# A short convolution and an ELU layer: softmax on eight partitions, one load of w_in, the band in contiguous rows

## The chip, the cores and the metric

The kernel runs on one core of one Trainium2 chip. Its metric is the time of one execution on the device in microseconds; lower is better.

## The reference

`x` is (8, 4096, 192), `weight` is (8, 7): eight heads of 24 channels, seven taps each. A softmax over each head's taps gives the weights of a causal convolution along the sequence. Its output, seen as 32768 tokens of 192 channels, goes through two matrix products with an ELU between them.

```python
w = softmax(weight, axis=-1)                      # (8, 7)
x_pad = concat([zeros(B, 6, D), x], axis=1)
a[b, s, h, :] = sum_k w[h, k] * x_pad[b, s + k, h, :]
h = a.reshape(32768, 192) @ w_in                  # w_in (192, 2048)
g = where(h > 0, h, exp(min(h, 0)) - 1)
out = g @ w_out                                   # w_out (2048, 192)
```

## The kernel before

Tokens are worked through in 32 stages of 1024 (`SUP`), each as two groups of 512. The hidden dimension is cut into 16 blocks of 128 (`NQ`). The counter `n` runs over stage and block, 512 values in all. For each `n` and each group `r` TensorE makes one hidden tile of 128 x 512 in a PSUM bank, out of three accumulating matmuls of 64 rows ("h", L798). Group 0 uses partitions 0 to 63 of `w_in` and `att`, group 1 partitions 64 to 127, so that two matmuls run side by side in the two halves of the array. This is why `w_in` stands twice in SBUF, in the lower and in the upper half of the partitions.

A hidden tile then goes through three engines. ScalarE takes the exponential from PSUM to `E` (L606), GpSimd clamps it (L557), and VectorE makes the ELU from `E` and the PSUM bank and writes `gT` (L679), which frees the bank. TensorE multiplies `gT` by `w_out` ("o", L821).

The convolution of stages 1 to 31 is done on TensorE as a product of windows of `x` (`xg`) with a banded matrix `Tm` ("c", L773), four units of two heads per stage. ScalarE evacuates each unit (L602), and a transposing DMA on SP's queue puts a stage into `att`. Stage 0 has its own way, so that it can start early: ScalarE casts `xs` (L585), TensorE transposes it ("t", L723), VectorE and ScalarE copy the transposed tiles into `xT`, and TensorE multiplies them by `taps`, one diagonal matrix for each tap ("d", L751).

`Tm` is made from the softmax. VectorE writes the weights into `wband`, SP's queue writes `wband` to the DRAM tensor `conv_band` with one element more per row than the row is long, and reads it back shifted (L844, L853). SP waits for the first transfer before it issues the second. The first convolution unit stands in TensorE's order at n = 6 (`EARLY_CONV`), and waits for both transfers.

The order of TensorE's items is written out when the program is built, from a plan with a cost for each kind of item; engines run their lists in order and wait on semaphores. At the start stand `WARM[0]` matmuls on zeros ("w", L714), then `start_up`: transposes with one more matmul on zeros after each of three, and the "d" matmuls. Before each of n = 1 to 3 stands one more.

GpSimd makes the masks (`ident`, `band16`) and then issues the loads, which all go through one queue in this order: `w_in` columns 0 to 1023 into both halves (six DMAs), half of `w_out`, two of `xg`, `w_in` columns 1024 to 2047 into both halves (six DMAs), the rest of `w_out`, two of `xg`. Each of these DMAs also changes float32 to a 16-bit type. The load of `weight` and that of eight rows of `x` (`xh`) are SP's first two; that of `xs` is on ScalarE's queue.

Of the kernel before, what the change touches and what calls it, by code (L numbers as in the profile page):

```python
# [5 lines left out]
ALU = mybir.AluOpType  # L6
# [6 lines left out]
P = 128  # L13
HP = 64
# [22 lines left out]
QB = 2  # L37
WARM = (15, 1)
FILL = 1
WCOLS = ((0, 8 * FC), (8 * FC, 16 * FC))  # L40
HALO = 8
# [15 lines left out]
def bass_lightweight_conv__then__act_elu_kernel(  # L57
# [178 lines left out]
    emit(tail)  # L236
    pe_order.append(("w", 0, WARM[0]))
    for what in start_up:
# [44 lines left out]
    with ExitStack() as stack:  # L283
        def sbuf(name, shape, dt):
            return stack.enter_context(nc.sbuf_tensor(name, shape, dt))
# [4 lines left out]
        def sema(name):  # L290
            return stack.enter_context(nc.semaphore(name))

        xg = sbuf("xg", [P, NXB, 2 * NWIN, D], BF16)
        Tm = sbuf("Tm", [P, HEADS, CW], BF16)
        ident = sbuf("ident", [P, P], BF16)
# [6 lines left out]
        xb = sbuf("xb", [P, 3, XI, HP], BF16)  # L302
        own = sbuf("own", [P, HEADS], FP32)
        band16 = sbuf("band16", [P, 2 * HEADS], FP32)
        wown = sbuf("wown", [P, HEADS], FP32)
        wsel = sbuf("wsel", [P, KSIZE, HEADS], FP32)

# [6 lines left out]
        osb = sbuf("osb", [P, 2, 2, 2, D], FP32)  # L314
        wq = sbuf("wq", [P, HEADS, KSIZE], FP32)
        wmx = sbuf("wmx", [P, HEADS], FP32)
        wq2 = sbuf("wq2", [P, HEADS, KSIZE], FP32)
        wex = sbuf("wex", [P, HEADS, KSIZE], FP32)
        wsum = sbuf("wsum", [P, HEADS], FP32)
        wrs = sbuf("wrs", [P, HEADS], FP32)  # L320
        wband = sbuf("wband", [P, HEADS, BW], BF16)
        wch = sbuf("wch", [P, KSIZE], FP32)
        zw = sbuf("zw", [P, TW * HEADS], BF16)
        scr = sbuf("scr", [P, 2], FP32)
        H = psum("H", [P, NBANK, GS])

        s_wq = sema("s_wq")
        s_w = [sema(f"s_w{i}") for i in range(4)]
        s_set = sema("s_set")
# [5 lines left out]
        s_xh = sema("s_xh")  # L335
        s_own = sema("s_own")
        s_wb = sema("s_wb")
# [132 lines left out]
        def _gpsimd(g: bass.BassGpSimd):  # L470
# [28 lines left out]

            def load_w_in(k, half):  # L500
                c0, c1 = WCOLS[k]
                for j in range(3):
                    g.dma_start(  # L503
                        w_in[HP * half : HP * (half + 1), j, c0:c1],
                        bass.AP(
                            tensor=moe_w_in.tensor,
                            offset=8 * j * FF + c0,
                            ap=[[CPH * FF, HEADS], [FF, 8], [1, c1 - c0]],
                        ),
                    ).then_inc(s_w[k], 16)  # L510

            def load_w_out(k):
                q = slice(NQ // 2 * k, NQ // 2 * (k + 1))
                g.dma_start(
                    w_out[:, q, :], moe_w_out.rearrange("(q p) d -> p q d", p=FC)[:, q, :]
                ).then_inc(s_w[2 + k], 16)

# [11 lines left out]
            for step in range(2):  # L529
                W(s_id, 2 + step)  # L530
                g.affine_select(
                    out=band16[:],
                    in_=band16[:] if step else ones[:, 0 : 2 * HEADS],
                    pattern=[[8 * (2 * step - 1), 2 * HEADS]],
                    compare_op=ALU.is_ge,
                    fill=0.0,
                    base=7 * step,
                    channel_multiplier=1 - 2 * step,
                ).then_inc(s_id)
            load_w_in(0, 0)  # L540
            load_w_in(0, 1)
            load_w_out(0)
            for gr in range(2):
                load_x(1, gr)
            load_w_in(1, 0)
            load_w_in(1, 1)
            load_w_out(1)
# [67 lines left out]
        def _vector(v):  # L615
            W = Waits(v)
            v.memset(zw[:], 0.0).then_inc(s_zw)  # L617
            v.memset(wband[:], 0.0).then_inc(s_wb)
            v.memset(xbh[:, :, 0, :], 0.0).then_inc(s_xz)
            W(s_wb, 1)  # L620
            W(s_id, 4)
            v.tensor_tensor(own[:], band16[:, 0:HEADS], band16[:, HEADS : 2 * HEADS], ALU.add).then_inc(s_own)
            W(s_wq, 16)
            v.tensor_reduce(wmx[:], wq[:], AXIS.X, ALU.max).then_inc(s_set)  # L624
            W(s_set, 1)
            v.tensor_tensor(  # L626
                wq2[:],
                wq[:],
                wmx[:, :].unsqueeze(2).to_broadcast([P, HEADS, KSIZE]),
                ALU.subtract,  # L630
            ).then_inc(s_set)
# [4 lines left out]
            W(s_set, 4)  # L636
            W(s_own, 1)
            v.tensor_tensor(wown[:], wrs[:], own[:], ALU.mult).then_inc(s_set)
            W(s_set, 5)
            v.tensor_tensor(  # L640
                wsel[:],
                wex[:, :, :].rearrange("p h k -> p k h"),
                wown[:, :].unsqueeze(1).to_broadcast([P, KSIZE, HEADS]),
                ALU.mult,
            ).then_inc(s_set)
            W(s_set, 6)
            v.tensor_reduce(wch[:], wsel[:], AXIS.X, ALU.add).then_inc(s_set)
            W(s_set, 7)
            v.tensor_tensor(  # L649
                taps[:],  # L650
                ident[:, :].unsqueeze(1).to_broadcast([P, KSIZE, P]),
                wch[:, :].unsqueeze(2).to_broadcast([P, KSIZE, P]),
                ALU.mult,
            ).then_inc(s_tap)
            for at, j in enumerate((3, 0)):
                W(s_xt, at + 1)
                v.tensor_copy(*transposed(j)).then_inc(s_fd)  # L657
            v.tensor_tensor(
                wband[:, :, P - KSIZE : P][:, :, ::-1],
                wex[:, :, :],  # L660
                wrs[:, :].unsqueeze(2).to_broadcast([P, HEADS, KSIZE]),
                ALU.mult,
            ).then_inc(s_set)
            W(s_first, 2)
            v.tensor_copy(*first_att(1, 0, GS)).then_inc(s_fd)  # L665
            W(s_first, 3)
            v.tensor_copy(*first_att(2, GS // 2, GS)).then_inc(s_fd)
            for item in dve_order:
                if item[0] == "e":
                    v.tensor_copy(*out_evac(W, *item[1:])).then_inc(s_od)  # L670
                    continue
                _, n, u = item
                i = unit_at[n, u]
                s, q = divmod(n, NQ)
                if s >= NG3:
                    for g in range(2):
                        W(s_fin[g], 2 * (s - NG3 + 1))
                W(s_clp, i + 1)
                v.scalar_tensor_tensor(  # L679
                    out=gT[:, s % NG3, q, u, :],  # L680
                    in0=E[:, i % NE, :],
                    scalar=1.0,
                    in1=H[:, bank_of[item], :],
                    op0=ALU.subtract,
                    op1=ALU.max,
                ).then_inc(s_tt)

        @block.tensor
        def _tensor(pe):
# [16 lines left out]
            for item in pe_order:  # L706
                if item[0] == "w":
# [5 lines left out]
                    for _ in range(item[2]):  # L713
                        pe.matmul(H[:, bank, :], zw[:, 0:P], zw[:, 0:GS], start=True, stop=True)  # L714
                elif item[0] == "t":
                    j = item[1]
# [26 lines left out]
                elif item[0] == "d":  # L743
                    j = item[1]
                    W(s_tap, 1)
                    first_evacuated(W, ("t", j))
# [12 lines left out]
                elif item[0] == "c":  # L759
# [9 lines left out]
                    else:  # L769
# [4 lines left out]
                        H[0:CW, bank_of["c", m], 256 * q : 256 * q + UC],  # L774
                        Tm[rows, h, :],
                        xg[rows, s % NXB, :, CPH * h : CPH * (h + 1)].rearrange(
# [8 lines left out]
                elif item[0] == "h":  # L785
                    _, n, r, j = item
                    s, q = divmod(n, NQ)
                    if j == 0:
                        if q < WCOLS[0][1] // FC:
                            W(s_w[0], 96)  # L790
                        else:
                            W(s_w[1], 96)
                        if s:
                            W(s_att[s % 2], att_need(s))
                        wait_bank(item[:3])
# [12 lines left out]
                else:  # L808
# [7 lines left out]
                    if visit is not None and not opens:  # L816
                        W(s_turn[g], turns[k, g])
                    W(s_w[2 + q // (NQ // 2)], 16)
                    W(s_tt, tt_count(NQ * t + q, g))
# [16 lines left out]
        def _sync(sy):  # L836
            W = Waits(sy)
            sy.dma_start(
                wq[:, :, :].rearrange("p h k -> p (h k)"),
                bass.AP(tensor=weight.tensor, offset=0, ap=[[0, P], [1, HEADS * KSIZE]]),  # L840
            ).then_inc(s_wq, 16)
            sy.dma_start(xh[:, :], x_flat[GS - HALO : GS, :]).then_inc(s_xh, 16)
            W(s_set, 8)
            sy.dma_start(  # L844
# [8 lines left out]
            sy.dma_start(  # L853
                Tm[:, :, :],
                band[:, P - 1 : P - 1 + HEADS * BW].rearrange("p (h i) -> p h i", h=HEADS)[
                    :, :, 0:CW
                ],
            ).then_inc(s_band, 16)

            sync_work = []  # L860
# [39 lines left out]
```

## Time and profile before

| | |
|---|---|
| median of 9 runs | 734.33 us (733.53 to 734.9) |
| the profiled execution's own time | 734.4 us |
| its span, first to last instruction | 732.5 us |
| busy: PE, DVE, ACT, POOL | 721.6, 639.9, 677.5, 671.2 us |
| mean granted TensorE clock | 0.995 |
| HBM read, written | 36.20 MB, 25.66 MB |

PE is TensorE's matmuls, PEld its weight loads, DVE VectorE, ACT ScalarE, POOL GpSimd, SP SyncE; a name with q is an engine's sequencer, which issues DMAs. An arrow `a <- b` in a row of the waits means that a waited for b; then come the total in us, the number of times and the longest. In a row of the chain or of the timeline stand start, length in us, engine, tile and line. A row of the windows gives the stretch, its length, the busy time and the count of each engine, the granted clock as a share of full speed, the time of the DMA packets as a share of 16 engines (over 1 where packets overlap), and GB/s. Matmuls are pipelined, so a busy TensorE may still work below its peak.

### The profile page before, as it was taken

The numbers are of one execution on the slowest core, as the hardware profiler recorded it, in microseconds if no ns is written. First come the engines' busy times: TensorE is split into PE (matmuls) and PEld (weight loads), VectorE is DVE, ScalarE is ACT, GpSimd is POOL, SyncE is SP. The second block draws the span as 40 slices with busy tenths as digits, with TensorE's granted clock in tenths as the row PEclk, the third lists the DMA queues.
The fourth block names the chain that finished last, engine by engine and source line by source line (L and its number), as shares of the span: only waits on it lengthen the run. The fifth ranks groups of instructions, "written<-read, shape, count | busy, mean of one in ns | idle before, by whom it ended". The sixth has DMA issues, their size and how long they took to land.

```text
span 732.5 us, 27618 instructions
## 1 busy us (share of the span) xinstructions
PE 721.6 (99%) x11858; PEld 683.0 (93%) x11860; DVE 639.9 (87%) x1042; ACT 677.5 (92%) x1287; POOL 671.2 (92%) x1116
## 2 busy tenths in 40 slices
PE   8799999999999999999999999999999999999998
PEld 4479999999999999999999999999999999999997
DVE  3699899889899889899889898889898889898993
ACT  4699999999999999999999999999999999999993
POOL 7699999999999999999999999999999999999892
PEclk9899999999999999999999999999999999999999
DMA  9635455434445534545534455534445533545212
GB/s 188 81 51 94 72 95 85 85 52 92 76 92 85 79 66 84 75 92 85 95 51 83 80 88 86 95 59 75 83 84 85 95 63 70 93 75 84 69 34 67
DMA packets 133947, 59.40 MB, mean 81 GB/s; under 512 B 100024, under 2 KB 132800, under 8 KB 133824
## 3 DMA queue, kind: packets, MB, share of 16 engines
q1 hardware_dynamic: 88960, 39.07, 23.6%
q0 software_dynamic: 44448, 17.58, 22.7%
q8 instruction: 93, 1.52, 0.9%
q10 hardware_dynamic: 416, 0.98, 0.4%
q14 instruction: 30, 0.25, 0.1%
HBM read 36.20 MB, written 25.66 MB: 84 GB/s over the span
## 4 chain that ended last, share of the span: by engine, by line
PE 93%; DMA 3%; POOL 2%; ACT 1%; DVE 1%; issue 0%; DVEq 0%
PE H L821 53%; PE H L798 37%; PE H L773 3%; POOL E L557 1%; DMA Tm<-conv_band 1%; DMA conv_band<-wband 1%; DMA wq<-in_weight_dram 1%; ACT E L606 1%; POOL xg L485 0%; ACT csb L602 0%; DVE taps L649 0%; ACT osb L610 0%; DVE gT L679 0%; DVE xT L657 0%; DVE osb L670 0%
## 5 line engine op out<-in xcount | busy, mean ns | idle before, releaser
L679 DVE SCALAR_TENSOR_TENSOR gT<-E,H 128x512 f16<-128x512 f32 x1024 | 633.3, 683 | 71.7 <-POOL E L557 70.3
L821 PE MATMUL H<-w_out,gT 64*128 64x192 f16 x8192 | 685.3, 243 | 0.2
L798 PE MATMUL H<-att,w_in 64*128 64x512 bf16 x3072 | 683.4, 377 | 0.6 <-issue 0.3
L557 POOL TENSOR_SCALAR E<-E 128x512 f32<-128x512 f32 x1024 | 607.7, 614 | 48.0 <-ACT E L606 37.0
L821 PEld LDWEIGHTS H<-w_out,gT 64*128 64x128 f16 x8192 | 628.3, 94 | 21.0 <-PE H L821 2.6
L606 ACT ACTIVATE E<-H 128x512 f32<-128x512 f32 x1024 | 593.7, 601 | 34.0 <-PE H L798 8.2
L798 PEld LDWEIGHTS H<-att,w_in 64*128 64x128 bf16 x3072 | 275.2, 93 | 6.7 <-ACT csb L602 1.0
L773 PE MATMUL H<-xg,Tm 64*112 64x240 bf16 x496 | 93.4, 268 | 4.7 <-DMA Tm<-conv_band 4.2
L602 ACT ACTIVATE csb<-H 112x480 bf16<-112x480 f32 x124 | 70.0, 564 | 0.0
L610 ACT ACTIVATE osb<-H 128x384 f32<-128x384 f32 x127 | 61.7, 486 | 7.5 <-PE H L821 7.4
L773 PEld LDWEIGHTS H<-xg,Tm 64*112 64x112 bf16 x496 | 58.0, 127 | 8.7 <-DMA Tm<-conv_band 4.5
L485 POOL DMA_DIRECT2D xg<-in_x_dram x63 | 56.1, 896 | 0.2 <-issue 0.2
L714 PE MATMUL H<-zw 128*128 128x512 bf16 x19 | 7.6, 549 | 1.5 <-DVE zw L617 1.5
L714 PEld LDWEIGHTS H<-zw 128*128 128x128 bf16 x21 | 2.6, 130 | 6.4 <-issue 4.6
L670 DVE COPY osb<-H 128x384 f32<-128x384 f32 x1 | 0.6, 558 | 8.4 <-PE H L821 8.4
L503 POOL DMA_DIRECT2D w_in<-in_moe_w_in_dram x12 | 7.1, 669 | 0.0
L751 PE MATMUL H<-xT,taps 128*128 128x512 bf16 (+1 forms) x28 | 4.7, 325 | 0.0
L751 PEld LDWEIGHTS H<-xT,taps 128*128 128x128 bf16 x28 | 2.7, 97 | 2.0
L597 ACT ACTIVATE att<-H 128x512 bf16<-128x512 f32 (+1 forms) x2 | 1.0, 490 | 3.7 <-PE H L751 3.7
L576 ACT ACTIVATE wex<-wq 128x56 f32<-128x56 f32 x1 | 0.2, 249 | 4.0 <-DVE wq L626 4.0
L665 DVE CAST att<-H 128x512 bf16<-128x512 f32 x1 | 0.7, 692 | 3.6 <-PE H L751 3.6
L624 DVE TENSOR_REDUCE wmx<-wq 128x8 f32<-128x56 f32 x1 | 0.2, 211 | 3.7 <-DMA wq<-in_weight_dram 3.7
(34 smaller groups left out, 19.2 us busy)
## 6 DMA issues: line engine op xcount, KB each, us to landing
out_dram<-osb SPq DMA_DIRECT2D x127, 192.0 KB, 3.6
xg<-in_x_dram POOLq DMA_DIRECT2D x61, 240.0 KB, 5.0
w_in<-in_moe_w_in_dram POOLq DMA_DIRECT2D x12, 128.0 KB, 8.1
xs<-in_x_dram ACTq DMA_DIRECT2D x1, 768.0 KB, 6.6
w_out<-in_moe_w_out_dram POOLq DMA_DIRECT2D x2, 384.0 KB, 11.3
att<-csb SPq DMA_TRANSPOSE x31, 4.3
conv_band<-wband SPq DMA_DIRECT2D x1, 480.0 KB, 6.8
Tm<-conv_band SPq DMA_DIRECT2D x1, 224.0 KB, 8.9
```

Source lines behind the costliest of these rows:

```text
L485: g.dma_start(xg[0:rows, b, 2 * w0 + gr : 2 * w1 : 2, :], src).then_inc(s_x[b][gr], 16)
L503: g.dma_start(w_in[HP * half : HP * (half + 1), j, c0:c1], bass.AP(tensor=moe_w_in.tensor, offset=8 * j * FF + c0, ap=[[CPH * FF, HEADS], ...
L557: g.tensor_scalar(out=E[:, i % NE, :], in0=E[:, i % NE, :], scalar1=1.0, scalar2=0.0, op0=ALU.min, op1=ALU.max,).then_inc(s_clp)
L602: a.activation(*conv_evac(W, m), ACT.Copy).then_inc(s_ce)
L606: a.activation(E[:, i % NE, :], H[:, bank_of[item], :], ACT.Exp).then_inc(s_exp)
L610: a.activation(*out_evac(W, *item[1:]), ACT.Copy).then_inc(s_oev[item[2]])
L679: v.scalar_tensor_tensor(out=gT[:, s % NG3, q, u, :], in0=E[:, i % NE, :], scalar=1.0, in1=H[:, bank_of[item], :], op0=ALU.subtract, op1=A ...
L714: pe.matmul(H[:, bank, :], zw[:, 0:P], zw[:, 0:GS], start=True, stop=True)
L751: ins = pe.matmul(H[:, bank_of[item] + part, c0:c1], taps[:, tap, :], xT[:, j, HALO - PAD + tap + c0 : HALO - PAD + tap + c1], start=(tap ...
L773: ins = pe.matmul(H[0:CW, bank_of["c", m], 256 * q : 256 * q + UC], Tm[rows, h, :], xg[rows, s % NXB, :, CPH * h : CPH * (h + 1)].rearrang ...
L798: ins = pe.matmul(H[:, bank_of[item[:3]], :], w_in[HP * r : HP * (r + 1), j, FC * q : FC * (q + 1)], att[HP * r : HP * (r + 1), s % 2, j, ...
L821: ins = pe.matmul(acc_of(k, g)[:, D * kb : D * (kb + 1)], gT[HP * rt : HP * (rt + 1), t % NG3, q, g, t0 : t0 + P], w_out[HP * rt : HP * (r ...
```

## The change

The softmax is computed once, on eight partitions, one for each head, instead of on all 128. Two small matmuls spread it: one with the mask `owner` gives every partition the seven weights of its head (for `taps`), one with ones and a block-diagonal copy `wnb` gives every partition all 56 weights (for `wband`). VectorE reads both from PSUM. `wband` is written right after `taps`, ahead of the copies into `xT`. The matmuls on zeros at the start are 6, then the two small ones, then 4.

`w_in` is loaded into the lower half only, in three parts (columns 0 to 511, 512 to 1023, 1024 to 2047). VectorE copies the first two parts to the upper half, the third goes by a DMA from SBUF to SBUF on SP's queue. The hidden matmuls of group 1 wait for these copies.

`Tm` has rows of 240 columns per head instead of 112, so that the read of the band moves one contiguous row of 1792 elements to each partition; the matmuls use the first 112 columns.

```diff
-WARM = (15, 1)
+WARM = (6, 1, 4)
-WCOLS = ((0, 8 * FC), (8 * FC, 16 * FC))
+WCOLS = ((0, 4 * FC), (4 * FC, 8 * FC), (8 * FC, 16 * FC))
...
-    pe_order.append(("w", 0, WARM[0]))
+    pe_order += [("w", 0, WARM[0]), ("s",), ("w", 0, WARM[2])]
...
-        Tm = sbuf("Tm", [P, HEADS, CW], BF16)
+        Tm = sbuf("Tm", [P, HEADS, BW], BF16)
-        wq = sbuf("wq", [P, HEADS, KSIZE], FP32)
+        wq = sbuf("wq", [HEADS, KSIZE], FP32)
-        zw = sbuf("zw", [P, TW * HEADS], BF16)
+        zw = sbuf("zw", [P, GS], BF16)
...
 # GpSimd: two masks for owner (as before for band16), one more for block8, then
-            load_w_in(0, 0)
-            load_w_in(0, 1)
+            load_w_in(0)
+            load_w_in(1)
             load_w_out(0)
             for gr in range(2):
                 load_x(1, gr)
-            load_w_in(1, 0)
-            load_w_in(1, 1)
+            load_w_in(2)
             load_w_out(1)
...
 # VectorE
+            def upper_half(v, k):
+                c0, c1 = WCOLS[k]
+                W(s_w[k], 48)
+                v.tensor_copy(w_in[HP:P, :, c0:c1], w_in[0:HP, :, c0:c1]).then_inc(s_wc)
 # wmx, wq2, wex (ScalarE), wsum, wrs as before but on 8 partitions; then
-            v.tensor_tensor(wown[:], wrs[:], own[:], ALU.mult).then_inc(s_set)
-            v.tensor_tensor(wsel[:], wex..., wown..., ALU.mult).then_inc(s_set)
-            v.tensor_reduce(wch[:], wsel[:], AXIS.X, ALU.add).then_inc(s_set)
+            v.tensor_scalar(out=wn[:], in0=wex[:], scalar1=wrs[:, 0:1], ...)
+            v.tensor_tensor(wnb[:], block8[:], wn..., ALU.mult).then_inc(s_set)
+            W(s_sel, 1)
             v.tensor_tensor(
                 taps[:],
                 ident[:, :].unsqueeze(1).to_broadcast([P, KSIZE, P]),
-                wch[:, :].unsqueeze(2).to_broadcast([P, KSIZE, P]),
+                H[:, bank_of["d", 2], 0:KSIZE].unsqueeze(2).to_broadcast([P, KSIZE, P]),
                 ALU.mult,
+            ).then_inc(s_tap)
+            v.tensor_copy(
+                wband[:, :, P - KSIZE : P][:, :, ::-1],
+                H[:, bank_of["d", 2], HP : HP + HEADS * KSIZE]...,
             ).then_inc(s_tap)
             for at, j in enumerate((3, 0)):
                 W(s_xt, at + 1)
                 v.tensor_copy(*transposed(j)).then_inc(s_fd)
-            v.tensor_tensor(wband[...], wex[...], wrs..., ALU.mult).then_inc(s_set)
+            upper_half(v, 0)
             W(s_first, 2)
             v.tensor_copy(*first_att(1, 0, GS)).then_inc(s_fd)
             W(s_first, 3)
             v.tensor_copy(*first_att(2, GS // 2, GS)).then_inc(s_fd)
+            upper_half(v, 1)
...
 # TensorE
+                elif item[0] == "s":
+                    W(s_id, 4)
+                    W(s_set, 6)
+                    pe.matmul(H[:, bank_of["d", 2], 0:KSIZE], owner[:, :], wn[:, :],
+                              start=True, stop=False)
+                    pe.matmul(H[:, bank_of["d", 2], HP : HP + HEADS * KSIZE],
+                              ones[0:HEADS, :], wnb..., start=False, stop=True).then_inc(s_sel)
...
-                        Tm[rows, h, :],
+                        Tm[rows, h, 0:CW],
...
+                        if r == 1 and part < 2:
+                            W(s_wc, part + 1)
+                        elif r == 1:
+                            W(s_wd, 16)
...
 # SP
-            W(s_set, 8)
+            W(s_tap, 2)
             sy.dma_start(conv_band ..., wband...).then_inc(s_band, 16)
             W(s_band, 16)
             sy.dma_start(
-                Tm[:, :, :],
-                band[:, P - 1 : P - 1 + HEADS * BW].rearrange(...)[:, :, 0:CW],
+                Tm[:, :, :].rearrange("p h i -> p (h i)")[:, 0 : HEADS * BW - P],
+                band[:, P - 1 : HEADS * BW - 1],
             ).then_inc(s_band, 16)
+            W(s_w[2], 48)
+            c0, c1 = WCOLS[2]
+            sy.dma_start(w_in[HP:P, :, c0:c1], w_in[0:HP, :, c0:c1]).then_inc(s_wd, 16)
```

## The prediction, made before the changed kernel ran

> **What bounds the kernel now.** I read the page's chain first, then the windows, to see whether a saving at the start reaches the end.
>
> ```profile
> PE 93%; DMA 3%; POOL 2%; ACT 1%; DVE 1%; issue 0%; DVEq 0%
> ```
>
> TensorE holds the end, and DMA's 3% is some 22 us of waiting in one place. All the edits work before n = 9, so I went to the chain in order of time, and from it to the waits of the first 60 us.
>
> ```profile
> 0.80 5.62 DMA wq<-in_weight_dram
> 6.44 0.22 DVE wmx L624
> ...
> 8.44 1.09 DVE taps L649
> 9.53 0.69 DVE xT L657 x2
> 10.38 6.85 DMA conv_band<-wband
> 17.24 8.87 DMA Tm<-conv_band
> 26.15 0.45 PE H L773
> ```
>
> ```profile
> DVE gT L679 <- POOL E L557: 9.3, 12, 3.9
> PE H L773 <- DMA Tm<-conv_band: 4.2, 1, 4.2
> ```
>
> The first chain of the kernel is weights, softmax, band write, band read: 25.3 us. TensorE reaches the first convolution unit (n = 6) at 21.9 and stands 4.2 us for Tm. What that costs shows in VectorE's gT instructions (window; length, busy, count, granted clock, DMA, GB/s); below it all engines (PE, PEld, DVE, ACT, POOL, then the clock), for the clock's fall:
>
> ```profile
> 17.70:25.10 7.40, 7.26 (x12) 0.92 1.36 181
> 25.10:28.90 3.80, 0.00 (x0) 0.50 0.55 65
> 28.90:38.50 9.60, 7.82 (x13) 0.90 0.19 37
> 38.50:46.00 7.50, 7.29 (x14) 1.00 0.08 18
> ```
>
> ```profile
> 23.00:24.00 1.00, 0.00 (x0) 0.00 (x0) 1.00 (x3) 0.00 (x0) 1.00 (x2) 0.99 1.38 172
> 24.00:25.00 1.00, 0.00 (x0) 0.00 (x0) 1.00 (x2) 0.00 (x0) 0.12 (x1) 0.50 1.47 179
> ```
>
> VectorE sets the pace here: 12 gT in 7.26 us, 0.605 each. It ran 3.1 us behind TensorE, so the stall reached it late: 3.8 us with nothing. Then, at half clock (0.50 until about 30.8), it did 12 full ones (the thirteenth only begins) in 9.6 us where 12 x 0.605 = 7.3 are enough: 2.3 us more. After 38.5 it is packed again, with 0.2 idle in 7.5. In the windows from 60 to 120 us TensorE is busy all the time (10.00 of 10.00), so what is lost before n = 20 is never regained. Price of the stall: 3.8 + 2.3 = 6.1, less 0.3 of the idle that packed stretches have too, 5.8 us; at least TensorE's own 4.2.
>
> **The softmax's start.** The weights were copied to 128 partitions (28 KB, landing 5.6 us after issue); now 8 rows of 28 bytes come. The trace has no such small load: the bounds are 2.0 us, the quickest landing of an out_dram store on the same queue, and 5.6. With 8 rows it is nearest to the quick end: I take 2.5, landing at 3.3 where it was 6.4. VectorE's memsets end by 2.6 in the old trace and the exponential's table is ready at 3.0, so neither is later.
>
> **The softmax's length.** Old: 6.44 to 10.38, 3.9 us. New: seven small steps (wmx, wq2, wex, wsum, wrs, wn, wnb) at the old spacing of 0.25 = 1.75; the two small matmuls and the hand-overs, 0.5 (L735's three of 8 columns take 0.21; at most 1.0); taps, same 128x896, now from PSUM, 1.1 to 1.3; the band's 56 columns 0.25, straight after taps instead of after two xT copies. Sum 3.7. The band write is issued at 3.3 + 3.7 = 7.0 instead of 10.4.
>
> **The band.** The write is unchanged: 6.85 (bounds 3.5, the median store, and 6.85): lands at 13.9. The read had 1024 rows of 224 bytes and took 8.87; now 128 rows of 3584 bytes, twice the bytes, in the number of rows and nearly the size of the write. I take the write's 6.85, bounds 3.5 and 8.87: Tm at 20.8 (17.4 to 22.8). TensorE asks at 21.9. The stall goes; 0.7 us more would be absorbed, because VectorE's 3.1 us of lag exceed the 2.4 us from TensorE's first hidden matmul (15.4) to the first gT (17.8). Worth 5.8.
>
> **x and the first attention.** What begins TensorE's own work is xs.
>
> ```profile
> 7.45 1.67 ACT L585 ACTIVATE xb<-xs 128x512 bf16<-128x512 f32 x3
> ...
> 10.70 4.74 PE L751 MATMUL H<-xT,taps 128*128 128x512 bf16 x28
> ...
> 15.37 1.07 PE L798 MATMUL H<-att,w_in 64*128 64x512 bf16 x6
> ```
>
> From xs (7.4) to the first hidden matmul (15.4) lies a fixed 8 us; taps (9.5, now about 6.7) are not on it. xs, 768 KB, shares the DMA engines with the 128 rows of wq until 6.4; DMA's share is 0.32 at 1.5 to 3 us and 0.82 at 4.5 to 6. Without them xs may land sooner: at most 2.0 us (768 KB at the 298 GB/s of 4.5 to 6 us is 2.6; begun at 1.8, plus 1 to land, 5.4), at least nothing. I take 0.6.
>
> **Warm-up.** 15 zero matmuls, 1.54 to 7.6, become 6, a wait for wnb, the two small ones, and 4. Six at the old spacing of 0.43 end at 3.9; wnb is ready at 3.3 + 1.75 = 5.1, and the 4 end at 5.6 + 1.7 = 7.3, before the transposes (8.1, less 0.6). All of TensorE's queue stands behind this wait. The risk is the clock: weight loads fall from 0.15 to 0.10 us at 7.0, after 5.4 us of unbroken work; now the longest unbroken stretch before is 2.6. If full speed comes only 5.4 us after the restart at 5.1, thus at 10.5, transposes and fills are slow: their 3.1 us of matmul (3 x 0.63 and 3 x 0.39) cost up to 3.1 more. If it comes by 7.5, nothing. I take 0.5.
>
> The Trainium skill (TensorE: Matmul & The Clock Gate, Part 1) has the full clock come after about 3.4 us of sustained work and go after an idle window of that length. Six matmuls alone would not reach it, so the rule speaks against the change; it would leave the transposes slow and put the sum near 730. But the trace shows the clock cut at 24.0 after only 2.1 us of idling, so less than that was enough here, and what part of a stretch must be busy no row tells.
>
> **w_in once.** Six of twelve loads go: 768 KB less in a stretch where the DMA engines are full from 6 to 26 us. GpSimd issues half the rows' bytes, 3 loads fewer (0.58 each, 1.7 us), after one more mask (0.2 to 0.5 later); nothing waits for it before 17.2. The first two parts are copied by VectorE, 64x1536 each. Not shown in the trace: below, 0.5 (the 536-word memset of zw); above, 2.1 (three times the 0.69 of the 128x512 copy). I take 1.0. The first lies in the 3.6 us in which VectorE waits before att (10.3 to 13.9), behind it only that att copy; the second between 15.9 and 17.8, 1.9 us, with the whole gT stream queued behind. At 2.1 it would cost 0.2. If the first part landed after 10.3, lateness would be paid one for one beyond 2.6 us; its loads are the first in the queue and half as large, so nothing.
>
> By the Trainium skill (VectorE: DVE Perf Modes, perf-mode tier table) a 16-bit copy within SBUF runs at four elements a cycle, an estimate of 0.6 us here; the sum would be the same, since both copies are hidden.
>
> **The last third part.** The upper copy of columns 1024 up goes by SP: behind the band read's issue, it waits for the load, and all the att transposes stand behind that wait (first at 35.6: harmless). Its reader is n = 8, two n after the first convolution: 21.9 - 0.6 + 2.4 = 23.7, with 0.7 us of slack 24.4. The load's last issue was at 10.7, landing a median 10.5 later in that stretch, at 21; now with 1.2 us earlier issue and half the bytes in front, 16.5 to 20. Copy: 384 KB, 3.5 to 6.85: between 20 and 27. I take 24.6, toward the late end because this stretch's loads are all slow: 0.2 lost.
>
> **Sum**, from the profiled execution's 734.4 (span 732.5 and 1.9 around it; the median of nine is 734.33): 734.4 - 5.8 - 0.6 + 0.5 + 0.2 = 728.7.
>
> **Rivals.**
> *The weights do not land sooner* (5.6 us again). For: a fixed part may dominate; xs is in flight too. Against: stores on this queue landed in 2.0. wnb is at 8.2, the 4 warm-ups end at 10.4, transposes start 2.3 late and slow (1.5 to 3.1, 2.2 taken); Tm lands at 24, in time for a TensorE that is as late. 734.4 - 5.8 + 2.3 + 2.2 = 733.1.
> *Cold clock*: attention's 4.74 us also run half-slow, 2 to 3 us on top of the transposes' 1.5: 731 to 733.
> *The stall moves from n = 6 to n = 8.* Tm is early, but the SP copy of w_in waits for a load at 20.5 and then takes the band read's 8.9: 29.4, which is 5.0 past 24.4, and 2.3 of half clock follow. 734.4 - 5.8 - 0.6 + 7.3 = 735.3; above the old time from a landing at 28.5 on, by over 0.2% from 30.0 on. Against: the DMA engines carry less by then; a landing at 26 to 27 costs 1.5 to 3 (730 to 732).
> *It does not do what it says*: Tm lands no earlier because the read has twice the bytes. The old pair took 15.7 us in full traffic; from 7.0 that ends at 22.7, 1.4 after a TensorE that asks at 21.3, 0.7 of it past the slack: 729.4. So an early start alone is nearly enough.
>
> **Chances.** Forecast 0.64, own range 727 to 730.5; weights late 0.10 (half of it within 0.2%); cold clock 0.11; stall at n = 8 0.15, of which 0.07 ends beyond 735.9. A difference under 0.2% (1.5 us) can't be told from none. Faster 0.83, same 0.09, slower 0.08. Range: from 726.5 (xs 2 us sooner) to 732.3, which takes in the milder rivals.
>
> **What would show it.** Right: conv_band issued near 7; Tm landed before 22, no row "PE H L773 <- DMA Tm"; the gT line packed from its start to n = 20; one clock of 1.00 from 10 us on; xb before 7.4. Wrong: L714's second group ending after 8; L751 much over 4.74; TensorE waiting at L798 for a DMA into w_in.

## The result and the profile after

The changed kernel takes 730.92 us (median of 9 runs, 730.26 to 732.0), the kernel before 733.93 in the same comparison (29 runs). The ratio is 0.996, 95% interval 0.9952 to 0.9968: 3.0 us faster. Forecast were 728.7, in a range of 726.5 to 732.3. Of the changed kernel's ten executions, five have a mean granted clock of 0.999 or 1.000 and take 730.3 to 730.9 us; five, the profiled one among them, have 0.998 and take 731.0 to 733.4.

The profiled execution of the changed kernel took 733.35 us (span 731.3), longer than any of the nine timed ones. Its profile therefore shows the mechanism at its largest, and what it costs is read from medians. The first lines are the page's chain by engine, then the chain of the first 60 us in order of time (start, length, what).

```profile
PE 94%; POOL 2%; ACT 1%; DVE 1%; issue 1%; DMA 1%; SPq 0%; DVEq 0%
```

```profile
1.27 4.28 DMA xh<-in_x_dram
5.58 0.36 ACT xbh L587
5.94 0.53 ACT xb L594
...
9.08 4.74 PE H L788 x28
...
16.18 4.88 DVE gT L699 x8
...
24.36 3.51 issue
```

DMA falls from 3% of the chain to 1%. Softmax, band write and band read, 25.3 us of the old chain, are gone from it; the start is now set by the load of xh and xs. But a new piece stands at 24.36: TensorE stands for 3.5 us at something that the chain only calls "issue". The waits of TensorE, then those of SP's queue, then the DMA issues say what it is.

```profile
PE H L837 <- issue: 3.5, 1, 3.5
PE H L810 <- DVE gT L699: 0.9, 1, 0.9
```

```profile
SPq L899 <- DMA w_in<-in_moe_w_in_dram: 11.2, 1, 11.2
SPq L892 <- DMA conv_band<-wband: 4.6, 1, 4.6
```

```profile
22.23 0.71 SPq L899 DMA_DIRECT2D w_in<-w_in  x1
```

```profile
w_in<-w_in SPq DMA_DIRECT2D x1, 384.0 KB, 5.6
```

L810, the first convolution, no longer waits for Tm. It waits 0.9 us for VectorE to free a bank, as it should in a stage that VectorE paces. L837 is the hidden matmul. SP waits 11.2 us for the load of the last third of w_in, issues the copy to the upper half at 22.2, and the copy takes 5.6: 27.8. At 27.9 TensorE goes on, with n = 8. The stall has moved from n = 6 to n = 8. VectorE's gT shows its size (window, length, busy, count, clock, DMA, GB/s), and the windows over all engines (the clock is the number before the last two) show the clock.

```profile
16.10:26.50 10.40, 9.83 (x16) 1.00 1.15 177
26.50:30.50 4.00, 0.01 (x2) 0.70 0.01 6
30.50:37.10 6.60, 5.16 (x9) 0.92 0.29 55
```

```profile
27.00:28.00 1.00, 0.12 (x3) 0.15 (x5) 0.00 (x0) 0.00 (x0) 0.00 (x0) 1.00 0.03 10
28.00:29.00 1.00, 1.00 (x9) 0.44 (x6) 0.00 (x0) 0.00 (x0) 0.00 (x0) 0.54 0.00 0
```

VectorE does nothing for 4.0 us and then 8 gT (the ninth only begins) in 6.6 us. The same eight take 5.7 us in a kernel without a stall (third_direct_warm6, below), so the stall costs 4.0 + 0.9 = 4.9 us. The old stall cost 4.7 by the same count, which the section on the prediction works out. In this execution the gain is no more than the earlier start: the first gT comes at 16.18 instead of 17.79.

### The profile page after: what moved, and what is told of

The parts are those of the page before. It is cut to its first block, busy times and chain, and to the rows that moved or that the text cites. A ratio compares the mean times of both kernels' runs of the same rounds, so it can differ in the third digit from the quotient of the medians.

```text
span 731.3 us, 27614 instructions
## 1 busy us (share of the span) xinstructions
PE 720.2 (98%) x11856; PEld 682.6 (93%) x11857; DVE 640.6 (88%) x1042; ACT 677.6 (93%) x1287; POOL 670.1 (92%) x1114
## 4 chain that ended last, share of the span: by engine, by line
PE 94%; POOL 2%; ACT 1%; DVE 1%; issue 1%; DMA 1%; SPq 0%; DVEq 0%
PE H L860 53%; PE H L837 37%; PE H L810 3%; POOL E L566 1%; ACT E L615 1%; DVE gT L699 1%; PE H L788 1%; DMA xh<-in_x_dram 1%; ACT csb L611 0%; POOL xg L485 0%; PE H L760 0%; ACT osb L619 0%; PE H L734 0%; DVE osb L690 0%; ACT xb L594 0%
## 5 line engine op out<-in xcount | busy, mean ns | idle before, releaser
L837 PE MATMUL H<-att,w_in 64*128 64x512 bf16 x3072 | 683.5, 377 | 4.1 <-issue 3.5
L860 PEld LDWEIGHTS H<-w_out,gT 64*128 64x128 f16 x8192 | 629.8, 94 | 20.2 <-PE H L860 2.3
L837 PEld LDWEIGHTS H<-att,w_in 64*128 64x128 bf16 x3072 | 274.8, 93 | 11.0 <-issue 4.6
L810 PE MATMUL H<-xg,Tm 64*112 64x240 bf16 x496 | 92.9, 267 | 1.1 <-DVE gT L699 0.9
L810 PEld LDWEIGHTS H<-xg,Tm 64*112 64x112 bf16 x496 | 57.3, 126 | 5.1 <-issue 1.8
L734 PE MATMUL H<-zw 128*128 128x512 bf16 x15 | 5.7, 483 | 1.2 <-DVE zw L632 1.2
L503 POOL DMA_DIRECT2D w_in<-in_moe_w_in_dram x9 | 5.3, 614 | 0.0
```

Source lines behind the costliest of these rows:

```text
L503: g.dma_start(w_in[0:HP, j, c0:c1], bass.AP(tensor=moe_w_in.tensor, offset=8 * j * FF + c0, ap=[[CPH * FF, HEADS], [FF, 8], [1, c1 - c0]], ...
L810: ins = pe.matmul(H[0:CW, bank_of["c", m], 256 * q : 256 * q + UC], Tm[rows, h, 0:CW], xg[rows, s % NXB, :, CPH * h : CPH * (h + 1)].rearr ...
L837: ins = pe.matmul(H[:, bank_of[item[:3]], :], w_in[HP * r : HP * (r + 1), j, FC * q : FC * (q + 1)], att[HP * r : HP * (r + 1), s % 2, j, ...
L860: ins = pe.matmul(acc_of(k, g)[:, D * kb : D * (kb + 1)], gT[HP * rt : HP * (rt + 1), t % NG3, q, g, t0 : t0 + P], w_out[HP * rt : HP * (r ...
```

## The experiments

Ratios are to the kernel before, with their 95% intervals. The first four take the suspected wait away, lengthen it, or put its cause alone into the kernel before.

**third_first**: the last part of w_in is loaded earlier.

```diff
             load_w_in(1)
+            load_w_in(2)
             load_w_out(0)
...
-            load_w_in(2)
             load_w_out(1)
```

> The changed kernel with one move: GpSimd issues the load of the last part of w_in (columns 1024 up) right after the first two, ahead of w_out and xg, so that SP's copy to the upper half can go out as soon as the band read is issued. Theory A (what is missing of the forecast's gain is TensorE standing at n = 8 for that copy, 3.5 us in the profile, and the slow clock after it): the copy is issued at about 11 us and lands by 19, no wait at L837 before 30 us, no stretch at clock 0.5, time 726.0 to 727.5, that is 3.5 to 5 us under the changed kernel's 730.9. Theory B (that wait costs nothing in the end, because the stage is held by VectorE or by the later order of work anyway): within 1 us of 730.9.

Measured: 729.71 us (728.38 to 730.3), ratio 0.9938 (0.9925 to 0.995). The profiled execution took 728.51. The copy is issued at 13.4, not 11, because SP still waits for the load, and takes 8.2 us, much longer than in the changed kernel, but it lands at 21.5, before n = 8. The wait at L837 is gone:

```profile
SPq L899 <- DMA w_in<-in_moe_w_in_dram: 2.2, 1, 2.2
```

Theory B falls. In size A is missed: even the fastest execution, 728.38, is above its range. The executions form two groups, two at 728.4 and 728.5 and three at 729.7 to 730.3.

**third_direct**: no copy by SP; the last part is loaded into both halves.

```diff
-            load_w_in(2)
+            load_w_in(2, 0)
+            load_w_in(2, 1)
...
-            W(s_w[2], 48)
-            sy.dma_start(w_in[HP:P, :, c0:c1], w_in[0:HP, :, c0:c1]).then_inc(s_wd, 16)
```

> The changed kernel without SP's copy: GpSimd loads the last part of w_in twice from HBM, into the lower and the upper half, at its place in the queue. Theory A (TensorE stands at n = 8 for the copy because it starts only when the load has landed and then takes 5.5 us): the upper half lands about 2 us after the lower one, at 21 to 24, TensorE waits 0 to 2 us, time 726.5 to 729. Theory B (the wait at n = 8 costs nothing): 730.9 within 1 us. Theory C (the traffic that was saved is what counts, so that loading it again loses): 732 or more.

Measured: 728.08 us (728.03 to 730.17), ratio 0.9923 (0.9911 to 0.9935). Both halves have landed at 23.4, and no wait at the hidden matmul exceeds 0.2 us. Theory A holds, B and C fall: 384 KB more to load cost nothing that shows, while the copy that saved them cost 2.8 us (730.92 against 728.08).

**third_last**: the last part is loaded later, after the second w_out and xg.

> The changed kernel with one move the other way: the load of the last part of w_in comes after the second w_out and xg loads. Theory A (TensorE's stand at n = 8 for SP's copy is paid one for one): the load lands at 25 to 26 instead of 22.2, the copy at 29 to 31.5, TensorE stands 5 to 7 us at L837, time 733.5 to 736, at or above the kernel before. Theory B (the wait at n = 8 is covered by other work): 730.9 within 1.

Measured: 734.32 us (733.4 to 735.26), ratio 1.0006 (0.9997 to 1.0015). The load lands at 25.0, the copy 3.7 us later at 28.7, sooner than expected; the queues are nearly empty by then (17 GB/s on average from 23.0 to 25.5). TensorE waits 2.9 us at L837 in the profile, less than expected: in that execution its start was 1.4 us later (first gT 17.6), for a reason that the warm-up experiment shows. The time is in A's range. The change with this one load moved gains nothing at all.

**w_in_once_only**: the kernel before, with the edits of w_in alone (three parts, the two copies on VectorE, the copy on SP).

> The kernel before with w_in loaded once alone: three parts, two copies on VectorE, the last by SP behind the band read; softmax, warm-up and band rows as before. The DMA engines carry 768 KB less, so Tm may land at 24 to 25 instead of 26.1, and the copy, issued at 18 to 21, at 25 to 27. Theory A (this part only adds a second wait behind the first): stall at n = 6 shorter by 1 to 2, a new one of 0 to 1.5 at n = 8: 732 to 734.5. Theory C (half the loads is what helps): 731 or less.

Measured: 733.49 us (732.54 to 734.75), ratio 0.9997 (0.9988 to 1.0006): no difference. Tm lands at 24.3 instead of 26.1, and TensorE still waits 2.7 us for it at n = 6; the copy lands at 25.9. Theory A holds.

The next three take the other parts one by one.

**w_in_twice**: the changed kernel with w_in loaded as before, thus softmax, warm-up and contiguous rows.

> The changed kernel with all of w_in loaded twice as before, in two parts, and no copies: the softmax on eight partitions, the shorter warm-up and the contiguous band rows alone. Theory A (these three bring the whole gain, the copies only cost): band issued at 5.7, Tm landed by 21, last part of w_in landed at 23 to 25, TensorE waits 1 to 2.5 us at n = 8, time 727.5 to 730, below the changed kernel. Theory C (half the loads is needed for Tm to be in time): Tm lands after 23, TensorE stands at L810 for it, 732 or more.

Measured: 728.23 us (727.83 to 729.76), ratio 0.9926 (0.9914 to 0.9938). Tm lands at 20.2, and no wait for it is left, nor the expected one at n = 8, in a profile whose start was late (first gT 17.9). This part of the change is worth 5.7 us; with the edits of w_in it is worth 3.0. Theory C falls. In the changed kernel the band write takes 5.0 us, here 7.2, so half the loads do make room, but only in slack: Tm is in time anyway.

**softmax_only**: w_in_twice with the band read in rows of 224 bytes.

> The softmax on eight partitions, the two small matmuls and the shorter warm-up alone: w_in loaded twice in two parts as before, the band read in rows of 224 bytes as before. Theory A (an early softmax alone brings the gain): band issued at 5.8, landed at 13, Tm 8.9 later at 22, TensorE asks at 21.2 to 22.8 and waits 0 to 0.8: 728 to 730, as w_in_twice. Theory D (the contiguous rows are needed for Tm to be in time): Tm at 24 or later, a wait at L810 of 1.5 us or more, 730 to 732.

Measured: 731.71 us (729.54 to 732.48), ratio 0.9971 (0.9962 to 0.9981). The wait for Tm is back, and the read is slow. The first line is TensorE's wait here, the second the DMA issue here, the third that of w_in_twice.

```profile
PE H L809 <- DMA Tm<-conv_band: 2.7, 1, 2.7
```

```profile
Tm<-conv_band SPq DMA_DIRECT2D x1, 224.0 KB, 10.7
```

```profile
Tm<-conv_band SPq DMA_DIRECT2D x1, 448.0 KB, 7.3
```

Twice the bytes in an eighth of the rows land 3.4 us sooner in the same traffic. Theory D holds: with this softmax, rows are worth 3.5 us (731.71 against 728.23).

**rows_only**: the kernel before with the contiguous rows alone.

```diff
-        Tm = sbuf("Tm", [P, HEADS, CW], BF16)
+        Tm = sbuf("Tm", [P, HEADS, BW], BF16)
...
-                Tm[:, :, :],
-                band[:, P - 1 : P - 1 + HEADS * BW].rearrange(...)[:, :, 0:CW],
+                Tm[:, :, :].rearrange("p h i -> p (h i)")[:, 0 : HEADS * BW - P],
+                band[:, P - 1 : HEADS * BW - 1],
```

> The kernel before with the contiguous band rows alone: each partition gets one row of 3584 bytes instead of eight of 224; softmax, warm-up and w_in as before. The band write is still issued at 10.4 and landed at 17.2. From softmax_only against w_in_twice (Tm 10.7 us after its issue with 224-byte rows, 7.3 with contiguous ones) theory D gives Tm at 24 to 25 instead of 26.1, a wait at L773 of 2 to 3 us instead of 4.2, time 731.5 to 733 against 733.8. Theory A (an early softmax alone brings the gain): no difference, 733.8 within 0.5.

Measured: 730.94 us (730.37 to 731.84), ratio 0.9963 (0.9951 to 0.9974). The read takes 7.0 us instead of 8.9 and lands at 23.5; the wait at L773 is 1.9. That is more than expected, and as much as the whole change. Of the 2.6 us by which Tm lands sooner, the read gives 1.8; the rest is the band write, which landed at 16.5 instead of 17.2 although the edit does not touch it. By medians rows alone bring 2.6 us, the softmax with the shorter warm-up 2.0, w_in alone nothing measurable, the first two together 5.7, all three 3.0.

Then the warm-up.

**third_direct_warm6**: third_direct with `WARM = (6, 1, 6)`.

> third_direct with 6 instead of 4 matmuls on zeros after the two small ones. In third_direct's executions there are two groups, four at 728.0 to 728.3 and one, the profiled, at 730.2; in the profiled one the weight loads of the transposes still take the slow 0.15 us and full speed comes at about 10.5 us, in the profile of third_first at 4.1, and the first hidden matmul comes 1.4 us apart. Theory K (the shorter warm-up leaves the clock unreleased in some executions, which costs 1.6 us in front of the first hidden matmul): with 6 the unbroken work reaches to 6.9, full speed comes by 7.5 in every execution, all of them at 727.8 to 728.9. Rival L (the two groups come from the DMAs): still two groups, 728 and 730.

Measured: 728.16 us (727.9 to 728.58), ratio 0.9926 (0.9912 to 0.9939): one group. Five executions are few for that, but the other runs say the same. With 4 matmuls on zeros, six of the fifteen executions of third_first, third_direct and w_in_twice lie at 729.6 or above, five of them with a mean clock of 0.999 or 1.000, thus without a stretch at half clock later on. With 6, none of the nine such executions of this kernel and of third_first_warm6 is above 728.9. The cause of the two groups shows in the transposes. The first line is from third_direct's profiled execution (730.17 us), the second from this one (728.16).

```profile
6.41 1.06 PE L761 MATMUL H<-ident,xb 64*64 64x64 bf16 x16
```

```profile
6.76 0.63 PE L761 MATMUL H<-ident,xb 64*64 64x64 bf16 x16
```

With the clock at half, 16 transposing matmuls take 1.06 us instead of 0.63, three times over, and each matmul on zeros between them 0.61 instead of 0.39; the first gT comes at 17.8 instead of 16.4. The first transposes take the same 1.06 in the late starts of w_in_twice, third_last and wide_load_beside, and 0.63 in the early one of third_first. Theory K holds. This kernel and third_direct, level with each other, are faster than the kernel before and the changed one. VectorE's gT in the stretches that answer to those above:

```profile
16.40:26.60 10.20, 9.69 (x16) 1.00 1.16 161
26.60:32.30 5.70, 5.10 (x9) 1.00 0.34 63
```

Eight gT in 5.7 us, 5.1 of them busy, where the changed kernel needed 4.0 + 6.6.

**changed_warm6**: the changed kernel with `WARM = (6, 1, 6)`.

> The changed kernel with 6 instead of 4 matmuls on zeros after the two small ones. Theory M (its own stall at n = 8 ends with SP's copy at a fixed moment, so the late clock of some executions is paid by a shorter stall, and an early clock gains nothing): 730.9 within 0.5, no second group. Rival N (the late clock costs it 1.6 us too, as it costs third_direct): 729.3 to 730.2.

Measured: 731.78 us (730.05 to 732.63), ratio 0.9971 (0.9962 to 0.9981). N falls: an early clock gains nothing here. It is above M's range too, and its interval overlaps that of the changed kernel, so whether it loses is not settled. Eight of its ten executions have a mean clock of 0.998 or less, against five of ten in the changed kernel. This suggests that after an early start the stand at n = 8 is more often long enough for the clock to be cut, but one trace of each kernel does not show it. The profiled execution (732.17) has full speed from the transposes on, the copy landing at 26.9, a wait of 2.2 at L837 and a second stretch at half clock from 26.8 on: what is won at the start is waited out at n = 8.

**third_first_warm6**: third_first with `WARM = (6, 1, 6)`.

> third_first (the last part of w_in loaded ahead of w_out and xg, the copy by SP kept) with 6 matmuls on zeros. Theory A with theory K (stall at n = 8 gone, clock always released early): all executions at 728.0 to 728.8, level with third_direct_warm6 at 728.2, three groups of 729.7 to 730.3 gone. Rival: SP's copy, landing at 21.5 in third_first, or xg behind the moved load holds TensorE in some executions: spread up to 730.3 as in third_first.

Measured: 728.7 us (727.97 to 730.42), ratio 0.9935 (0.9922 to 0.9949). Four of six executions are at 728.0 to 728.8; two are at 730.3 and 730.4, with a mean granted clock of 0.998 where the others have 1.000. A with K holds for the four alone. The profiled one (728.81) shows what the rival named: L810 waits 1.0 us for xg, whose load now stands behind the moved one. That the two slow ones were such a wait made longer, with a cut of the clock, was not seen in a trace.

Last, why xs landed earlier.

**wide_load_beside**: the old load of the weights to 128 partitions is added on SP's queue, behind the small one.

> The changed kernel with the old load of the weights to 128 partitions issued on SP's queue as well, right after the new small one, into a tile that nothing reads. Theory X (the 128 rows of that load held xs back): xs lands at 6.5 to 7.4 instead of 5.4, the first hidden matmul starts 1.1 to 1.6 us later, at 14.9 to 15.4. The time then moves by less than that, 0 to 0.8 us up, because the stall at n = 8 ends with SP's copy at the same moment and becomes shorter by as much. Rival Y (xs was earlier for another reason, such as chance): xs at 5.4, first hidden matmul at 13.8, time as the changed kernel within 0.4.

Measured: 730.93 us (730.1 to 733.5), ratio 0.9964 (0.9951 to 0.9976). xs landed at 5.4, so X's number was missed. But the added load was no fair stand-in: behind the small one it landed at 5.6, after xs. The first hidden matmul was late for another reason, the clock (full at 10.6). The time is that of the changed kernel although the first gT came 1.7 us later than in the latter's profile. In this profile (730.1) the copy landed at 26.0 and no wait at n = 8 exceeds 0.2 us: what the late start cost, the stall did not.

**wide_first**: the same load, put ahead of the small one.

> The changed kernel with the old load of the weights to 128 partitions put ahead of the new small one on SP's queue, so that it stands first, as in the kernel before; nothing reads its tile. Theory X (these 128 rows held xs back, by 2.1 us): xs lands at 7.0 to 7.5 instead of 5.3 to 5.6, ScalarE's cast of xs begins at 7.0 or later. Rival Y (xs is earlier for another reason, the later w_in loads or chance): xs at 5.3 to 5.8. The small load is then late too (5 to 6.5), the softmax with it, so the time is no test: 732 to 735.

Measured: 732.95 us (732.41 to 733.61), ratio 0.9992 (0.9982 to 1.0001). xs landed 5.6 us after its issue, at 6.4: between 5.4 (changed kernel) and 7.4 (before), below X's range and above Y's. By this one profile the 128 rows explain about 1.0 of the 2.1 us. That is a rough figure, since with the small load alone xs landed anywhere from 5.3 to 6.1 in the other profiles. The rest stays open; the loads of w_in, which begin at 2.4 here and in the changed kernel and at 1.85 in the kernel before, were not moved by themselves.

## Why the prediction was right, and where its size was off

- **Range: held by its wide end.** The median, 730.92, lies outside my own range of 727 to 730.5. The stated range holds it because it took in the milder rivals, and one of these came true.
- **Direction and first wait: right.** The band write was issued at 5.7 (forecast 7.0), Tm landed at 18.6 (20.8), and the wait at n = 6 is gone. Without SP's copy the forecast's sum is 734.4 - 5.8 - 0.6 + 0.5 = 728.5; third_direct and third_direct_warm6 measured 728.1 and 728.2.
- **That the two agree is partly luck.** I priced the first stall at 5.8, of which 2.3 for half clock, because I took 12 x 0.605 = 7.3 us as enough for the twelve gT that follow it. The same twelve (13th to 24th) take 8.7 us in third_direct_warm6, which has no stall (the count of 13 takes in the end of the one before):

```profile
23.60:32.30 8.70, 7.61 (x13) 1.00 0.46 69
```

- So half clock cost 9.6 - 8.7 = 0.9, and the stall 3.8 + 0.9 = 4.7 us. The start gave more than I took: the first gT comes 1.4 us earlier there (16.4 instead of 17.8), where my terms for xs and the clock come to 0.1. 734.4 - 4.7 - 1.4 = 728.3, so one error paid for the other. third_direct's profile, with its first gT at 17.8 as before and no stall, agrees: 730.17, 4.2 under 734.4.
- **The last third part is the step that failed.** I let the copy land at 24.6, for 0.2 us; it landed at 27.8 in the profile, past my bound of 27. The load that it waits for had landed only at 22.2, where I had 16.5 to 20. I had started from the median of the loads in that stretch, 10.5 us, but SP waits for the last of three. The first line is from the kernel before, the second from the changed one, each over all loads of w_in in the start:

```profile
DMA to landing us min/median/max: 5.8/8.1/11.8
DMA to landing us min/median/max: 2.7/4.1/12.3
```

- The three loads of the last part took 9.2, 9.5 and 12.3 us in the changed kernel. By medians the step costs 2.8 us; between the two kernels with 6 matmuls on zeros it is 3.6 (731.78 against 728.16). The rival "the stall moves from n = 6 to n = 8", with 0.15, is what happened, in its milder form, which I priced at 730 to 732. The sign of being wrong that I named, TensorE standing at the hidden matmul for a DMA into w_in, is there.
- **xs was mis-sized.** 0.6 taken, 2.1 measured (7.4 to 5.4), at the edge of the bound. Of these, 1.6 reached TensorE: ScalarE's cast moved from 7.45 to 5.85, the first hidden matmul from 15.37 to 13.75.
- **Clock: bounds right, value a mixture.** The cost is not 0.5 but about 0 or about 2 (728.0 to 728.3 against 730.17), by execution. The changed kernel seems to hide it, because what comes later at the start is subtracted from the wait at n = 8 (wide_load_beside). In the Trainium skill (TensorE: Matmul & The Clock Gate, Part 1) the window of 3.4 us runs free of the kernel, so that the moment of full speed varies from run to run; the two groups agree with that. Six matmuls on zeros can be enough: the four that follow the two small ones take 1.04 us in the changed kernel's profile, from 4.38 on, and 1.89 in third_direct's, from 4.41 on. So the clock was full 3.1 us after the first matmul (1.25) in the one, and not in the other.
- **Small terms.** wq landed at 2.15 (3.3). The softmax from there to the band's issue took 3.6 (3.7). The band write took 5.0 (6.85), its read 7.9 (6.85, bounds 3.5 and 8.87). VectorE's copies took 0.68 each in the changed kernel (1.0 taken) and were hidden; my estimate from the Trainium skill (VectorE: DVE Perf Modes, perf-mode tier table) was 0.6. Of the twelve loads of w_in three went and six were halved; the prediction's "six of twelve" is wrong, its 768 KB right.
- **The reason behind rows was weak.** I gave the contiguous read the write's duration and treated the rows as a detail beside the softmax; the runs show rows to be worth at least as much alone (2.6 and 2.0 us, with intervals that overlap).

## What to carry to other kernels

When a wait is taken away, list the next readers in program order and when each of their transfers can land: here a gain of 5.7 us was halved by a copy that a queue issued only after a load. Where a transfer waits for several loads, take the last of them and not the median. In this stretch a copy that saved traffic bought nothing, and it added a dependent transfer whose lateness had to be paid. To price a stall, compare with the same work in a kernel without one, not with the tightest spacing. The clock's two levels made groups of times here, so single profiles should be compared with the spread in mind.

## What the runs showed of the hardware that was not expected

- A load of 8 rows of 28 bytes landed 1.35 us after its issue; one of 128 rows, all reading the same 224 bytes, 5.6 (4.3 to 5.6 in five profiles).
- Reading 448 KB in 128 rows of 3584 bytes took 6.1 to 8.6 us in the first 25 us of these kernels, reading 224 KB in 1024 rows 6.8 to 10.7. In the changed kernel's profile no packet of SP's queue moved between 10.8 and 14.5, after the read was issued at 10.7, while GpSimd's queue was full; the other form waited as long (issued at 13.1 in softmax_only, none until 16.8).
- The same copy of 384 KB within SBUF took 3.7 us in nearly idle queues (third_last) and 8.2 in full ones (third_first).
- The clock was cut 2.1 us after TensorE went idle in the kernel before (21.9 to 24.0), and in the changed one only at 28.1, when TensorE, idle from 24.4, had been at work again for 0.2 us. It stayed at half for 3.4 us in the changed kernel (28.1 to 31.5) and for 6.8, twice as long, in the kernel before (24.0 to 30.8).
